# Transfers of block 2 respaced, q of batch 3 in two places, q's turn moved within its slot, and the last pair's sums and reads rerouted in an attention and MLP kernel

## The chip, the cores and the metric

The kernel runs on one core of one Trainium2 chip. The metric is the device time of the whole launch in microseconds; lower is better. The engines are named as in the profile: PE (TensorE) multiplies matrices, PEld is its weight load, DVE is VectorE, ACT is ScalarE, POOL is GpSimd, SP is SyncE, whose queue issues nearly all transfers here ("SPq"). Each engine works through its own list of instructions in the order in which the program put them; a wait at the head of a list holds all that is behind it.

## The reference

Everything is float32. There are 8 batches with 8 heads, 576 tokens and a head size of 64.

```python
kv  = einsum('bhsd,bhse->bhde', k, v)
out = einsum('bhsd,bhde->bhse', q, kv)
x   = out / sqrt(mean(out*out, -1) + 1e-6) * g_norm      # per head
x   = x.transpose(0, 2, 1, 3).reshape(4608, 512)
h   = x @ w_in                                            # 512 x 2048
g   = maximum(0.01 * h, h)
return g @ w_out                                          # 2048 x 512
```

## The kernel before, in words

The 4608 rows of x are worked through in nine blocks of 512 tokens (`NB` = 9, `NT` = 512). Blocks 0 and 1 have forms of their own. Blocks 2 to 8 all have the same form, in which both products are done by Strassen's method, at two levels where it pays, so that sums of operands on DVE and POOL take the place of matmuls.

**Slots.** A block from 2 on is a loop over four parts of the hidden size (`c`) and seven products of each (`t`), 28 slots, `slot = 7 * c + t`. A slot takes about 3.3 us of PE. It issues, in this order: one step of the first product h (`h_steps`, `product_h_two`), then at `t == 0` the tail of the part before (`h_before`: the sums that make g, the leaky ReLU on ACT and the sums of g, `sums_of`), then one step of the second product o (`go_o`, with a lag), then pieces of the tail of the last batch (`late`) and of the attention for the next block (`a_steps`), then up to two queued loads (`load_some`). What was put off with `put_off` runs at a later slot's start. The order on each engine is pinned to this order.

**A step of h.** Each step multiplies into two banks of PSUM, and its result is added by DVE or copied by ACT into `qs`, a region of the tile `w1_all`. A bank is used again two steps later, so that a result has about one slot to be taken out. The steps of one part are 1, 2, 6, 5, 7, 3, 4.

**Weights of h.** They lie in DRAM as sums made in block 1 and are read through a ring of five places in `w1_all` (`read`, line 748): after a step the read for the step five later is issued. One read is 128 x 896 floats (448 KB).

**Weights of o.** The sums of w_out lie in DRAM too (`w2_dram`). `sides_w2` makes and writes them in block 1; `read_side` (line 944) reads 128 x 512 floats into one of three places in the tile `pairs`, in the order of `side_reads`; `load_four` (lines 911 to 913) reads quarters for the two-level form and, in block 2, has POOL sum them and writes the sums back. The second product of block 1's last part, `product_o(3)`, runs during block 2's slots 4 to 13 and, when it has ended, issues three side reads and two times `load_four` at once. A pair of parts (`product_o_pair`) follows it.

**Attention of the next batch.** While block i runs, batch i + 1 is prepared. The four pairs of heads of q come in one after another: four transfers each (line 172), a turn on DVE (line 467, a transpose of 128 x 576) into the tile `qT`, and then the next pair's load. For batches from 3 on all q pairs use a single place, `q_in`, so that a load waits for the turn of the pair before. `attention_kv` multiplies k and v; the tail (`tail_of`, `outputs`, `both_outputs`) multiplies qT with kv into `o_ps`, and DVE and ACT normalise it into xT. The tables `FINE_2` (for block 2), `FINE_3` (for block 3) and `FINE_SLOTS` say how many steps of the attention follow each slot:

```python
    FINE_SLOTS = {4: 1, 8: 2, 11: 1, 15: 3, 16: 1, 17: 2, 18: 2, 19: 9}
    FINE_3 = {4: 1, 8: 2, 11: 1, 15: 3, 16: 1, 18: 2, 19: 3, 20: 9}
    FINE_2 = {2: 1, 5: 2, 8: 1, 11: 3, 16: 1, 17: 2, 18: 2, 19: 9}
```

In blocks 3 to 6 the four turns are the first step at slots 4, 8, 11 and 15. In block 2 they are at slots 2, 5, 8 and 11.

**The end.** The last pair of parts of block 8 has one level only and follows `LAST_PLAN` ("1a 2a 1b 2b 6a 6b 5a 5b ..."). It needs the four sums of g (`gs`) of the last part, which POOL makes (line 644, called from `sums_of`).

Of the kernel before, what the change touches and what calls it, by code (L numbers as in the profile page):

```python
# [24 lines left out]
def kernel(  # L25
# [112 lines left out]
        return ins.tile([P, J, D], F32, tag=f"{name}_in", name=f"{name}_in")  # L138

    def q_tile(b, p):  # L140
        if p % 2 and b < 3:
            return w1_all[:, 2 * NC * NW:]
        return ins.tile([P, T * D], F32, tag="q_in", name="q_in", bufs=1)

# [2 lines left out]
    def load_some(n=1):  # L147

        while to_load and n > 0:
            b, p, what = to_load.popleft()  # L150
            load_pair(b, p, what)
            n -= 1
# [306 lines left out]
    def attention(b, apart=True, fine=False):  # L459

        qT = qTs[b] = work.tile([P, NP, S], F32, tag="qT", name="qT")
        beside = b > KV_BESIDE
        kv_ps = None if beside else kv_tiles()

        def turn(p):
            q_in = q_ins.pop((b, p))
            in_turn(nc.vector.transpose(
                qT[:, p, :].rearrange("p (t s) -> p s t", s=T),
                q_in.rearrange("p (s d) -> p s d", d=D)[:, :, :32]))

        def load_q(p):
            n = NP * b + p + (1 if b > 2 else 2)
            if apart and n < NP * B and (b != 2 or n <= NP * 3):
                put_off(b > 2, lambda: to_load.appendleft((n // NP, n % NP, "q")))

        for m in range(2):
            turn(2 * m)
            load_q(2 * m)
            yield
            turn(2 * m + 1)  # L480
            load_q(2 * m + 1)
            if m:
                yield
            if kv_ps:
                attention_kv(b, m, [t[:, m, :] for t in kv_ps])
            if not apart and m == 0:
                for p in (2, 3):
                    load_pair(b, p)
            elif apart and not beside:
                load_kv(b + m, 2 - 2 * m)  # L490
            yield
            if apart:
                if m and kv_ps:
                    copy_kv(b, kv_ps)
                yield
        if not apart:
            copy_kv(b, kv_ps)
            yield
        kv = [(None, None), (None, None)]
        if KV_BESIDE <= b < B - 1:  # L500
            kv = [(None, 0), (None, 1)] if b == KV_BESIDE else \
                [(None, 0) if b == KV_BESIDE + 1 else (0, None), (1, None)]
        tails = [tail_of(b, max(i * NT, b * S), min((i + 1) * NT, (b + 1) * S), fine, kv[i - b])
                 for i in (b, b + 1)]
        last_tails[b] = tails[1]
        yield from tails[0]
# [133 lines left out]
            round_w(j)  # L640


    def add(eng, out_, a, b_, minus=False, pinned=False):
        ins = eng.tensor_tensor(out_, a, b_, op=ALU.subtract if minus else ALU.add)  # L644
        if pinned or steady:
            pin(ins)
# [23 lines left out]
    def sides_w2(n):  # L670

        c = n % NC
        b11, b12 = w2_sb[0][c][:, :, :N2], w2_sb[0][c][:, :, N2:]
        b21, b22 = w2_sb[1][c][:, :, :N2], w2_sb[1][c][:, :, N2:]

        def sums(i):
            t = (t12, t34)[i]
            if n >= NC:  # L680
                pin(nc.sync.dma_start(t, w2_dram[c][i]))
                return
            if i == 0:
                add(nc.gpsimd, t[:, 0], b12, b11, True)
                add(nc.gpsimd, t[:, 1], b22, t[:, 0], True)
            else:
                add(nc.gpsimd, t[:, 0], b22, b12, True)
                add(nc.gpsimd, t[:, 1], b21, t12[:, 1], True)
            if (n, i) == (NC - 1, 1):

                writes.append((w2_dram[c][i], t))
            else:
                pin(nc.sync.dma_start(w2_dram[c][i], t))
        return {1: b11, 2: b21, 3: b22, 5: t12[:, 0], 6: t12[:, 1], 7: t34[:, 0],
                4: t34[:, 1]}, sums
# [156 lines left out]
    def sums_of(c, to):  # L852

        g11, g21, g22, g12 = g_of(c)
        s1, s2, s3, s4 = (gpool.tile([P, 4, P], F32, tag=f"gs{i}", name=f"gs{i}")
                          for i in range(1, 5))
        to.update({1: g11, 2: g12, 3: s4, 4: g22, 5: s1, 6: s2, 7: s3})
        add(nc.gpsimd, s1, g21, g22)
        add(nc.gpsimd, s2, s1, g11, True)
        add(nc.gpsimd, s3, g11, g21, True)  # L860
        add(nc.gpsimd, s4, g12, s2, True)

    def product_h(c, w_sides, x_sides, to):

        g11, g21, g22, g12 = g_of(c)

        def done(i, bank):

            if i == 1:
                nc.scalar.copy(g11, bank)  # L870
            elif i == 5:
                nc.scalar.copy(g22, bank)
            elif i == 2:
                add(nc.vector, g11, bank, g11, pinned=True)
                relu(g11)
            elif i == 6:
                nc.scalar.copy(g21, bank)
            elif i == 3:
                add(nc.vector, g21, bank, g21, pinned=True)
                relu(g21)  # L880
            elif i == 7:
                add(nc.vector, g22, bank, g22, pinned=True)
                relu(g22)
            else:
                relu(g12, bank)

        yield from strassen((("ha", "hc"), ("hb", "hd"))[c % 2], lambda i, part, r: w_sides[i][:, part, r, :],
                            lambda i, part, r: x_sides[i][:, r, :], done)
        sums_of(c, to)

# [33 lines left out]
        put_off(3, sums)  # L926
        put_off(6, write)

    later, tick = [], 0

    def put_off(n, what):
        later.append((tick + n, what))
        later.sort(key=lambda x: x[0])

    side_reads = [(m + h, i) for m in range(NC, END, 2)
                  for i in ((5, 6, 7) if two_levels(m) else (6, 5, 7, 4)) for h in range(2)]
    side_at = {key: view(pairs, (16 + 4 * (at % 3)) * P, U, N2) for at, key in enumerate(side_reads)}
    to_read = collections.deque(side_reads)

    def read_side():  # L940
# [55 lines left out]
    def product_h_two(i, c, quarters, to, second):  # L996
# [46 lines left out]
        yield  # L1043
        for t in (g11, g12, g22, g21):
            relu(t)
        sums_of(n, to)

    def product_o(n, g_sides, os, finish):

# [10 lines left out]
        def done(i, bank):  # L1060
            key, fresh = into[i]
            to = os[key].rearrange("p u (v n) -> p (u v) n", v=2)
            if c == 0 and fresh:
                nc.scalar.copy(to, bank)
            else:
                add(nc.vector, to, bank, to)
            if c == NC - 1 and i in (2, 7, 3, 4):
                finish(key, os[key])

            if i == 5:  # L1070
                sums(0)
            elif i == 4:
                sums(1)


        yield from strassen((("oa", "oc"), ("oc", "oa"))[n % 2], lambda i, part, r: g_sides[i][:, 2 * r + part, :],
                            lambda i, part, r: w_sides[i][:, r, :], done)
        if n == NC - 1:
            for _ in range(3):
                read_side()  # L1080
            for m in range(2):
                load_four(NC + m)

    PLAN = "1a 1b . 5a 5b 6a 6b 3a 3b 7a 7b A D ."
    LAST_PLAN = "1a 2a 1b 2b 6a 6b 5a 5b 7a 7b 3a 3b 4a 4b"
# [1 line left out]
    def product_o_pair(n, g_sides, os, finish):  # L1087
# [36 lines left out]
        for step in (PLAN if two else LAST_PLAN).split():  # L1124
# [39 lines left out]
                           stop=(r == 1), skip_group_check=True)  # L1164
            if i in (5, 6, 7, 4):
                read_side()
            if h == 0:
                yield
                continue
# [107 lines left out]
    A_SLOTS = (2, 3, 5, 8, 10, 11, 13, 14, 15, 17)  # L1277

    TAIL_SLOTS = {1: 1, 4: 1, 5: 2, 6: 1, 8: 2}
    FINE_SLOTS = {4: 1, 8: 2, 11: 1, 15: 3, 16: 1, 17: 2, 18: 2, 19: 9}  # L1280
    FINE_3 = {4: 1, 8: 2, 11: 1, 15: 3, 16: 1, 18: 2, 19: 3, 20: 9}
    FINE_2 = {2: 1, 5: 2, 8: 1, 11: 3, 16: 1, 17: 2, 18: 2, 19: 9}
    SUM_SLOTS = {22: 2, 23: 1, 24: 1}

    LAG = 2
# [18 lines left out]
    for i in range(1, NB):  # L1304
        one = i == 1
        steady = not one
        late = last_tails.pop(i, iter(()))
        a_steps = attention(i + 1, fine=not one) if i + 1 < B else iter(())
        os = {}
        for c in range(NC):  # L1310
# [7 lines left out]
            for t in range(7):  # L1318
                slot = 7 * c + t
                tick += 1  # L1320
                while later and later[0][0] <= tick:
                    later.pop(0)[1]()
                go(h_steps, 1)
                if t == 0:
                    go(h_before, 3)
# [9 lines left out]
                if not one:  # L1335

                    go(late, TAIL_SLOTS.get(slot, 0))
                    go(a_steps, {2: FINE_2, 3: FINE_3}.get(i, FINE_SLOTS).get(slot, 0))
                    if i + 1 < NB:
                        if slot == 22:  # L1340
                            x_sides, new_quarters, sums, inner = sides_x(i + 1)
# [2 lines left out]
                            inner(0)  # L1344
                        elif slot == 26:
                            inner(1)
                    load_some(2 if i == 2 else 1)

                if c % 2 == 0 and now - 2 in begun and 2 <= t < 6:
                    inner_g(now - 2 + t % 2, 3 if t < 4 else 2)  # L1350
# [5 lines left out]
                if one:  # L1356
# [12 lines left out]
                        in_line = False  # L1369
                    if slot in A_SLOTS:  # L1370
                        go(a_steps, 1)
                    load_some(2 if i == 2 else 1)
                    if slot == 24:
                        go(a_steps)
                        x_sides, new_quarters, sums, inner = sides_x(i + 1)
# [13 lines left out]
            if one:  # L1389
                go(h_steps)  # L1390
            elif now == END - 1:
                for _ in range(2):
                    go(h_steps, 1)
                    go_o()
                go(h_steps)
            else:
                h_before = h_steps
            if c == NC - 1 and i + 1 < NB:
# [39 lines left out]
```

## Time and profile before

| what | value |
|---|---|
| median of 3 runs | 921.16 us (918.72 to 923.7) |
| the profiled execution's own time | 920.61 us |
| its span, first to last instruction | 918.9 us |
| granted TensorE clock | 1.000 |
| PE busy | 906.7 us, 99% of the span |
| DVE, ACT, POOL busy | 581.6, 329.2, 474.8 us |
| mean rate of all transfers | 224 GB/s, 206.25 MB |

The table of waits shows, for each engine and line, how long it stood idle and what ended that. The timeline shows instructions in order of time: start, duration, engine, line, operation, tiles out<-in, shape, count, and in brackets the idle time of the engine before it and what ended it. A row of SPq is a transfer's issue, not its duration.

### The profile page before, as it was taken

The page shows a single profiled execution, that of the slowest core. Times are in us where ns is not written, and L with a number is a line of the kernel's source. Part 1 is how long each engine was busy: PE and PEld are TensorE (multiplying, and loading weights), DVE is VectorE, ACT ScalarE, POOL GpSimd, SP SyncE. Part 2 cuts the span into 40 slices and gives each one's busy share as a digit, 9 for nine tenths or more (in the row PEclk, how much of TensorE's full clock was granted, in tenths as well). Part 3 has the DMA queues.
Part 4 walks back from the last instruction along what each step waited for, and adds up shares of the span by engine and source line. Part 5 has one row for each costly group of instructions (what it writes and reads, how often), then busy time and mean ns, then how long its engine had stood idle before and what let it go on. Part 6 is the DMA issues. An engine that isn't in the chain of part 4 may idle for free.

```text
span 918.9 us, 18517 instructions
## 1 busy us (share of the span) xinstructions
PE 906.7 (99%) x7148; PEld 774.8 (84%) x7148; DVE 581.6 (63%) x882; ACT 329.2 (36%) x645; POOL 474.8 (52%) x588
## 2 busy tenths in 40 slices
PE   8999999999999999999999999999999999999998
PEld 4444448888988989898999999999989899999997
DVE  5876985565865667665775576656755664555442
ACT  5454524332234232434333343334242524232420
POOL 2000246977539674656355653566266736673622
PEclk9999999999999999999999999999999999999999
DMA  8999918954799678967897679766876667667613
GB/s 255 216 246 235 246 61 263 363 182 154 245 281 359 192 243 273 293 206 245 230 293 234 211 235 290 251 196 212 235 235 203 184 203 234 195 196 229 209 41 103
DMA packets 102615, 206.25 MB, mean 224 GB/s; under 512 B 11264, under 2 KB 46976, under 8 KB 102528
## 3 DMA queue, kind: packets, MB, share of 16 engines
q1 hardware_dynamic: 98592, 199.50, 72.7%
q10 hardware_dynamic: 3488, 4.39, 1.4%
q8 instruction: 57, 0.93, 0.4%
q0 software_dynamic: 448, 1.18, 0.3%
q14 instruction: 30, 0.25, 0.1%
HBM read 176.72 MB, written 28.31 MB: 223 GB/s over the span
## 4 chain that ended last, share of the span: by engine, by line
PE 89%; DMA 4%; DVE 4%; issue 1%; POOL 1%; ACT 0%; SPq 0%; DVEq 0%; ACTq 0%; POOLq 0%
PE o_a L121 18%; PE o_c L121 15%; PE h_hd L121 9%; PE h_hc L121 9%; PE h_ha L121 9%; PE h_hb L121 8%; PE o_acc L121 6%; PE h_ps L121 6%; PE o_ps L121 3%; PE h_a L121 2%; PE h_b L121 2%; DMA q_in<-in_q_dram 1%; DVE g L644 1%; PE h_d L121 1%; PE h_c L121 1%; PE kv_ps L121 1%
## 5 line engine op out<-in xcount | busy, mean ns | idle before, releaser
L644 POOL TENSOR_TENSOR gs<-g 128x512 f32<-128x512 f32 x64 | 83.3, 1303 | 164.4 <-DVE w_all L644 79.6
L644 POOL TENSOR_TENSOR w_all<-w_all 128x512 f32<-128x512 f32 x28 | 56.2, 2008 | 120.2 <-ACT w_all L1021 114.1
L121 PE MATMUL o_a<-pairs,gs 128*128 128x256 f32 x480 | 114.0, 380 | 0.7 <-POOL gs L644 0.7
L836 ACT ACTIVATE g<-g 128x512 f32<-128x512 f32 x124 | 75.2, 629 | 74.6 <-DVE g L644 74.5
L644 DVE TENSOR_TENSOR g<-g,w_all 128x512 f32<-128x512 f32 (+1 forms) x84 | 92.6, 1102 | 6.9 <-POOL w_all L644 1.2
L121 PEld LDWEIGHTS o_a<-pairs,gs 128*128 128x128 f32 x480 | 86.9, 190 | 10.6 <-POOL gs L644 0.9
L644 DVE TENSOR_TENSOR o_all<-o_a,o_all 128x512 f32<-128x512 f32 (+1 forms) x53 | 35.4, 668 | 82.2 <-PE o_a L121 81.6
L644 DVE TENSOR_TENSOR o_all<-o_c,o_all 128x512 f32<-128x512 f32 (+2 forms) x80 | 46.5, 581 | 53.0 <-PE o_c L121 40.3
L1021 ACT COPY w_all<-h_hc 128x512 f32<-128x512 f32 x42 | 25.0, 596 | 116.2 <-PE h_hc L121 116.2
L121 PE MATMUL o_c<-pairs,gs 128*128 128x256 f32 x272 | 64.2, 380 | 1.8 <-DMA pairs<-w 1.8
L644 DVE TENSOR_TENSOR w_all<-h_ha,w_all 128x512 f32<-128x512 f32 x42 | 28.8, 686 | 52.0 <-PE h_ha L121 51.9
L121 PE MATMUL o_a<-w,g 128*128 128x256 f32 x248 | 58.8, 379 | 0.0
L121 PE MATMUL h_ps<-xT,w_all 128*128 128x512 f32 (+1 forms) x136 | 58.1, 571 | 0.3 <-DVE w_all L271 0.3
L121 PE MATMUL o_acc<-w,g 128*128 128x512 f32 x128 | 57.6, 594 | 0.0
L121 PE MATMUL o_c<-w,gs 128*128 128x256 f32 x240 | 56.6, 379 | 0.0
L644 POOL TENSOR_TENSOR pairs<-w 128x512 f32<-128x512 f32 x4 | 5.3, 1334 | 98.6 <-ACT cut L258 98.6
L644 DVE TENSOR_TENSOR g<-w_all 128x1024 f32<-128x1024 f32 x28 | 35.1, 1254 | 33.2 <-ACT w_all L1021 33.2
L121 PEld LDWEIGHTS o_c<-pairs,gs 128*128 128x128 f32 x272 | 49.5, 190 | 7.5 <-POOL gs L644 2.0
L121 PEld LDWEIGHTS h_ps<-xT,w_all 128*128 128x128 f32 x136 | 25.4, 190 | 29.0 <-issue 25.6
L121 PEld LDWEIGHTS o_acc<-w,g 128*128 128x128 f32 x128 | 24.2, 190 | 30.5 <-issue 29.9
L121 PEld LDWEIGHTS o_a<-w,g 128*128 128x128 f32 x248 | 45.0, 190 | 5.0
L121 PEld LDWEIGHTS o_c<-w,gs 128*128 128x128 f32 x240 | 43.5, 190 | 4.7
(262 smaller groups left out, 2292.4 us busy)
## 6 DMA issues: line engine op xcount, KB each, us to landing
w_all<-w SPq DMA_DIRECT2D x196, 448.0 KB, 4.4
pairs<-w SPq DMA_DIRECT2D x99, 256.0 KB, 3.7
v_in<-in_v_dram SPq DMA_DIRECT2D x29, 288.0 KB, 4.9
k_in<-in_k_dram SPq DMA_DIRECT2D x28, 288.0 KB, 4.9
q_in<-in_q_dram SPq DMA_DIRECT2D x48, 144.0 KB, 5.5
q_in<-in_q_dram SPq DMA_DIRECT2D x48, 140.0 KB, 5.8
w<-stage SPq DMA_DIRECT2D x12, 512.0 KB, 4.3
out_dram<-o_all SPq DMA_DIRECT2D x24, 256.0 KB, 5.6
```

The lines of the kernel that those rows point to most:

```text
L121: pin(nc.tensor.matmul(*args, **kw))
L644: ins = eng.tensor_tensor(out_, a, b_, op=ALU.subtract if minus else ALU.add)
L836: nc.scalar.activation(t, t if src is None else src, func=AF.Prelu, alpha=SLOPE)
L1021: nc.scalar.copy(q[:, at], bank)
```

## The change

It has five parts.

- **Block 2's transfers.** One queued load goes out in each slot, where block 2 had two. The three side reads and the two `load_four` that followed `product_o(3)` are issued within it, after its products 5, 7, 3 and 4. Both writes of the last part's sums of w_out to DRAM are put off to slot 4; one of them was issued in block 1's order before.
- **q of batch 3.** Its pair 1 gets a place of its own, in `w1_all`, which later holds part of `qs`. It is loaded in block 1, so that pairs 0 and 1 are both there at block 2's start. `load_q` queues the next load at once, not a slot later. In block 2 the turns move to slots 2, 3, 8 and 12, the two rounds of `attention_kv` to slots 4 and 12, and the tail's outputs to slots 17 and 18.
- **Turn first.** The tables get a second half, whose steps run ahead of the slot's h step. In blocks 3 to 6 the turns of slots 8, 11 and 15 run ahead of the h step and the o step of these slots; the one of slot 4 is now the first thing of slot 5.
- **Sums of the last pair.** For the last part the four sums of g are made by DVE, two and two, with DVE's other work between them.
- **Reads of the last pair.** The last five side reads go to places in `w1_all` and are all issued after step 1b, where they went round the three places of `pairs`.

```diff
     def q_tile(b, p):
-        if p % 2 and b < 3:
+        if p % 2 and NP * b + p < NP * 3 + 2:
             return w1_all[:, 2 * NC * NW:]
...
         def load_q(p):
-            n = NP * b + p + (1 if b > 2 else 2)
-            if apart and n < NP * B and (b != 2 or n <= NP * 3):
-                put_off(b > 2, lambda: to_load.appendleft((n // NP, n % NP, "q")))
+            n = NP * b + p
+            n += 2 if n <= NP * 3 else 1
+            if apart and n < NP * B and n != NP * 3 + 2 or n == NP * 3 + 2 and p == 0:
+                to_load.appendleft((n // NP, n % NP, "q"))
...
-            if m:
+            if m or b == KV_BESIDE:
                 yield
...
-            if (n, i) == (NC - 1, 1):
+            if n == NC - 1:
                 writes.append((w2_dram[c][i], t))
...
-        add(nc.gpsimd, s1, g21, g22)
-        add(nc.gpsimd, s2, s1, g11, True)
-        add(nc.gpsimd, s3, g11, g21, True)
-        add(nc.gpsimd, s4, g12, s2, True)
+        eng = nc.gpsimd if c < END - 1 else nc.vector
+        if c == END - 1:
+            yield
+        add(eng, s1, g21, g22)
+        add(eng, s2, s1, g11, True)
+        if c == END - 1:
+            yield
+        add(eng, s3, g11, g21, True)
+        add(eng, s4, g12, s2, True)
...
+    side_at.update((key, view(w1_all, 4 * at * P, U, N2)) for at, key in enumerate(side_reads[-5:]))
...
+            if n == NC - 1:
+                if i in (5, 7):
+                    read_side()
+                elif i == 3:
+                    load_four(NC + 1)
+                elif i == 4:
+                    read_side()
+                    load_four(NC)
...
-        if n == NC - 1:
-            for _ in range(3):
-                read_side()
-            for m in range(2):
-                load_four(NC + m)
...
+            if not two and step == "1b":
+                for _ in range(5):
+                    read_side()
...
-    FINE_SLOTS = {4: 1, 8: 2, 11: 1, 15: 3, 16: 1, 17: 2, 18: 2, 19: 9}
-    FINE_3 = {4: 1, 8: 2, 11: 1, 15: 3, 16: 1, 18: 2, 19: 3, 20: 9}
-    FINE_2 = {2: 1, 5: 2, 8: 1, 11: 3, 16: 1, 17: 2, 18: 2, 19: 9}
+    FINE_SLOTS = {16: 1, 17: 2, 18: 2, 19: 9}, {5: 1, 8: 2, 11: 1, 15: 3}
+    FINE_3 = {16: 1, 18: 2, 19: 3, 20: 9}, {5: 1, 8: 2, 11: 1, 15: 3}
+    FINE_2 = {4: 2, 8: 1, 12: 1, 13: 1, 17: 1, 18: 2, 19: 9}, {2: 1, 3: 1, 12: 1}
...
+                go(a_steps, 0 if one else fine[1].get(slot, 0))
                 go(h_steps, 1)
...
-                    go(a_steps, {2: FINE_2, 3: FINE_3}.get(i, FINE_SLOTS).get(slot, 0))
+                    go(a_steps, fine[0].get(slot, 0))
...
-                    load_some(2 if i == 2 else 1)
+                    load_some()
...
             elif now == END - 1:
-                for _ in range(2):
-                    go(h_steps, 1)
+                for steps in (1, 1, 2, 1, 1):
+                    go(h_steps, steps)
                     go_o()
-                go(h_steps)
```

More of the change, by code (lines that the diff above doesn't have):

```diff
@@ L640, in first_attention, with put_off @@
             round_w(j)
+    later, tick = [], 0
+    def put_off(n, what):
+        later.append((tick + n, what))
+        later.sort(key=lambda x: x[0])
     def add(eng, out_, a, b_, minus=False, pinned=False):
@@ L888, in product_h @@
                             lambda i, part, r: x_sides[i][:, r, :], done)
-        sums_of(c, to)
+        yield from sums_of(c, to)
     more = consts.tile([P, 19, P], F32, name="more")
@@ L927, in load_four @@
         put_off(6, write)
[L929 to L933, printed above, removed]
     side_reads = [(m + h, i) for m in range(NC, END, 2)
@@ L1045, in product_h_two @@
             relu(t)
-        sums_of(n, to)
+        yield from sums_of(n, to)
     def product_o(n, g_sides, os, finish):
@@ L1306 @@
         steady = not one
+        fine = {2: FINE_2, 3: FINE_3}.get(i, FINE_SLOTS)
         late = last_tails.pop(i, iter(()))
@@ L1371 @@
                         go(a_steps, 1)
-                    load_some(2 if i == 2 else 1)
+                    load_some()
                     if slot == 24:
```

## The prediction

> **What bounds the kernel now.** I read the page first: PE is busy for 906.7 of 918.9 us at a granted clock of 1.000, and 89% of the chain that ended last is PE. The change removes no matmul: on PE only the two rounds of kv matmuls and the o_ps products of block 2 stand elsewhere. So all that it can gain is PE's idle time, and the second view is the table of what PE waited for, without the first 27 us.
>
> ```profile
> PE o_c L121 <- DMA pairs<-w: 1.8, 1, 1.8
> ...
> PE h_ha L121 <- DVE w_all L644: 1.4, 1, 1.4
> PE o_ps L121 <- DVE qT L467: 1.3, 2, 0.7
> ...
> PE o_a L121 <- POOL gs L644: 0.7, 1, 0.7
> ```
>
> Columns: total us, times, longest. These four are the whole price: 5.2 us, 0.57% of the run. The third view is the timeline around each. Two lie in block 2:
>
> ```profile
> 266.17 1.89 PE L121 MATMUL o_c<-pairs,g 128*128 128x256 f32 x8
> ...
> 267.27 1.26 DVE L467 STREAM_TRANSPOSE qT<-q_in 128x576 f32<-128x576 f32 x1 [4.64 <-DMA q_in<-in_q_dram]
> ...
> 269.50 0.49 PE L121 MATMUL h_ha<-xT,w_all 128*128 128x128 f32 x2 [1.43 <-DVE w_all L644]
> ...
> 276.10 1.39 SPq L944 DMA_DIRECT2D pairs<-w  x3
> ...
> 282.16 1.97 PE L121 MATMUL o_c<-pairs,gs 128*128 128x256 f32 x8 [1.79 <-DMA pairs<-w]
> ```
>
> In the first, DVE stood 4.64 us at the turn of batch 3's last q, behind which the results of h were queued. In the second, PE wanted a side read that was issued only at 276.10. Matmul ends are modelled, so I count from starts: 8 records of 0.216 us each from 266.17 end at 267.90, and the next started at 269.50: 1.60 us lost. The second is 1.96 likewise (6 records of 0.112 from 279.53, next at 282.16).
>
> The third group is in blocks 4 to 6, at slot 16; block 5:
>
> ```profile
> 568.77 0.55 DVE L644 TENSOR_TENSOR w_all<-h_hd,w_all 128x384 f32<-128x384 f32 x1
> ...
> 569.72 1.26 DVE L467 STREAM_TRANSPOSE qT<-q_in 128x576 f32<-128x576 f32 x1 [0.41 <-DMA q_in<-in_q_dram]
> ...
> 571.04 0.63 PE L121 MATMUL o_ps<-qT,kv 64*32 64x128 f32 x20 [0.56 <-DVE qT L467]
> ```
>
> The fourth is at the end, where PE waits for POOL's second sum:
>
> ```profile
> 897.16 0.28 DVE L644 TENSOR_TENSOR o_all<-o_hc,o_all 128x128 f32<-128x128 f32 x1
> ...
> 898.53 1.26 POOL L644 TENSOR_TENSOR gs<-gs,g 128x512 f32<-128x512 f32 x1
> ...
> 899.85 1.13 PE L121 MATMUL o_a<-pairs,gs 128*128 128x256 f32 x4 [0.70 <-POOL gs L644]
> ```
>
> **Part 1, the last q turn of block 2: -1.6 us.** Pair 1 of batch 3 is now loaded in block 1, so that block 2 loads two pairs where it loaded three. Pair 2 is issued after the first turn (240.8) and pair 3 after the turn at slot 8. DVE is through slot 8's o result at 257.66 before; one turn (1.25) no longer stands ahead of it there, so the third turn ends at about 257.7 and pair 3 is issued then. A q pair lands 5.5 us after issue in the median and 8.7 at most: 263.2 to 266.4. Its turn is first in slot 12. The results behind it (0.68 and 0.55 us) must be out when slot 14's h starts, which is 267.9 without the stall: the turn must start by 267.9 - 1.23 - 1.26 = 265.4. Bytes: from 240.4 to 258 SP now issues some 6.2 MB (q, seven ring reads, two k and v pairs, two writes of 512 KB, out, two side reads), and 295 GB/s was moved in that stretch before, 413 in the best 4 us of block 2. At 295 the 6.2 MB and pair 3's 0.57 MB are through at 240.4 + 22.9 = 263.3, 2 us in time. What is late next is nothing at slot 14: the kv round behind slot 12's h has its k and v from slots 4 and 5.
>
> **Part 2, the side reads: -1.96 us.** They go out behind slots 7, 8 and 13, some 20 us ahead of their use; even the third, behind pair 0 of batch 4, needs only half its lead. `load_four` goes out behind slots 11 and 13 and its POOL sums at slots 14 and 16, ahead of POOL's add into qs at slot 14. If the first of them lands late, that add waits. By the bytes (2.4 MB from 258, at 295) it lands at about 266, before POOL needs it (270.05 before, about 268 now). Nothing, unless it lands after 270.
>
> Late next at that place would be POOL's last gs, done at 281.94 before; but PE's first product there uses the sums of the part before, done at 262.2, and the next one's first sum was done at 278.14. Nothing.
>
> **Part 3, turns first in blocks 3 to 6: -1.7 us.** Each load of the next pair goes a slot earlier (turn and queueing), and at slot 11 it passes the four `load_four` reads on SP. In block 5 the last turn follows the sum that ends at 568.26, not the two h results behind it: it ends at about 569.5, before PE asks at 570.04. The turn delays those results by 1.26 us to about 570.8; their bank is wanted at slot 17, 572.80. The stalls go: 1.3 in the table, 0.08 in block 4, and by starts up to 1.9. I take 1.7.
>
> The new wait is DVE's for q. Earliest is slot 8: in block 4 the pair lands at 446.46 and DVE comes there at 445.8, so DVE stands 0.7 us; behind it the results of slot 8, due at slot 10, 452.08; done by 449.1. Covered by 3 us.
>
> **Part 4, the end: -0.8 us.** DVE is free of the 1b results at 897.44. Two sums on DVE at 0.69 each (the row of g, 128x512 from SBUF, 0.69) end at 898.8; PE asks at 898.98 (898.53 and 4 records of 0.112). POOL has nothing left then. The one o_c result behind them is 1.4 us later (899.5); its bank is wanted at 901.7. The stall was 0.87 by starts; between 0.7 and 0.87 goes. The five reads were never waited for: 0.
>
> The Trainium skill speaks against this part ("Perfetto Trace Analysis", Optimizing Scalar/DVE Operations): VectorE and GpSimd share a port, so that moving work between them might not help. By it this part would be 0; here POOL's last other add ends at 893.2, so that there is nothing to share the port with.
>
> **Part 5, what block 2's start adds: +0.3 us.** At slots 2 and 3 two turns now stand one behind the other, ahead of the results of slot 4. They come after this:
>
> ```profile
> 234.53 5.14 DVE L431 TENSOR_TENSOR sum<-sq 128x192 f32<-128x192 f32 x2 [0.71 <-ACT sq L429]
> 239.59 1.24 DVE L467 STREAM_TRANSPOSE qT<-q_in 128x576 f32<-128x576 f32 x1
> ```
>
> Two small sums took 5.14 us, while POOL ran adds without a gap from 228.6 to 238.9. So the second turn ends at 242.1. ACT's copy of h_hd of slot 3 overwrites part of that q place and now waits for it (0.5 us, 242.6); PE wants this bank in slot 5, at 241.24 + 1.2 for the kv round that moved ahead = 242.45. Between 0 and 0.4; 0.3. The DVE results of slot 4 follow at 243.3, due at 244.94.
>
> The Trainium skill ("SBUF — State Buffer", Who interferes with whom) has the pair of ports held for one instruction of whichever engine came first. By it the sum would have waited only for the add that ran until 234.82, both turns would end near 238 and this term be 0; the row shows a wait through four adds.
>
> **What costs nothing.** Block 1 gets one q pair more and other places for POOL's sums and SP's writes. PE waited for nothing there (no row of the table lies between 140 and 226 us), and the cover is wide: the sums of g that PE takes up at 217.7 were done at 210.2. The write that held SP until 233.62, waiting for POOL, goes behind the ring reads of slots 0 to 2, so that these leave some us earlier; PE waited for none of them. If the cover is gone, PE pays one for one.
>
> **Sum.** 1.6 + 1.96 + 1.7 + 0.8 - 0.3 = 5.76 us, taken as 5.8; by the bounds 1.6 + 1.96 + 1.3 + 0.7 - 0.4 = 5.2 to 1.6 + 1.96 + 1.9 + 0.87 = 6.3. The profiled execution took 920.61, 0.55 below the median of 921.16. Against it: 914.8 us, 914.3 to 915.4.
>
> **Rivals.**
>
> *The transfers collide again, or DVE's start of block 2 does (0.27).* For: DMA engines are at a share of 0.91 from 240 to 258 already, and more now goes there. Pair 3 after 265.4 costs PE one for one; at the longest landing, 8.7, and an issue at 258.5 that is 1.8, more than part 1's 1.6, which is then gone: 916.4. If POOL's unbroken adds begin 2 us later, because the order of its sums in block 1 is another, part 5 is 2.3: 916.8; both, 918.4. Against: bytes and POOL's rows above.
>
> *It doesn't do what it says (0.05).* The stalls are only handed on to the next wait, as PE comes earlier to the same reads: 918.6 to 922.
>
> *Slower (0.06): the turns hold DVE.* In blocks 3 to 6 three turns now stand ahead of h results. Their place is slot 8, where the pair has the shortest lead. It decides from the point where q lands after 449.5 in block 4 (11.3 us after its issue at 438.19; 8.3 there before): then 449.5 + 1.26 + 1.37 passes 452.08, and each us costs one in each of four blocks. Landing 15 us after issue, 3.7 late, costs 14.8 against the 5.8: 930. It passes the break-even at 1.5 late. Against: 8.7 is the longest landing of q in the run.
>
> **How the numbers follow.** Forecast 0.62, at 914.8. Range 911.9 to 919: below, 914.3 less the 2.4 by which the lowest run shown lies under its median; above, the first rival's 918.4 and some of the second's. Some 0.12 is left out. About 0.5% (4.6 us) is what a measurement here can tell from no change; the forecast's 5.8 is just over it, and the first rival's cases are within. Faster 0.62, same 0.32, slower 0.06.
>
> **What would show it.** Right: the four rows of the first table gone, and PE busy 906.7 in a span near 913; the turn at slot 12 of block 2 with no wait for q over 1 us; at the end o_a following o_hc without a gap. Wrong: a row of PE waiting for ACT or DVE w_all near 242 (part 5 too small), a row for q or w_all near 268 (part 1), PE waiting for h results at slot 10 of blocks 3 to 6 (the slower rival), or pairs<-w still waited for.

## The result, and the profile after

The changed kernel took 914.65 us (median of 6 runs, 912.53 to 915.9) where the kernel before took 921.88 (6 runs on the same chip, 918.72 to 924.85): a ratio of 0.9918, with a 95% interval of 0.9893 to 0.9943. The profiled execution of the changed kernel took 914.69, with a span of 913.0 us, 5.9 less than before, at the same granted clock of 1.000. PE is busy for 905.2 us (906.7 before). By the medians the change is worth 7.2 us, by the two profiled executions 5.9; what follows accounts for the 5.9. One execution of one experiment, its profiled one (the first try with the end's sums on POOL), ran at a granted clock of 0.851 and took 1036.94 us; it is left out below.

The forecast was 914.8. Its sum was right, its terms were not: one was too small by 1.3 us, and a wait of 1.2 us that it had set at nothing ate nearly all of the difference. The table of what PE waited for, first for the changed kernel:

```profile
PE idle_ps L121 <- DVE group L307: 1.5, 1, 1.5
PE h_hb L121 <- ACT w_all L1342: 1.0, 1, 1.0
PE kv_ps L121 <- DMA pairs<-in_v_dram: 0.7, 1, 0.7
...
PE o_ps L121 <- DMA v_in<-in_v_dram: 0.3, 1, 0.3
```

All four rows that the prediction priced are gone. Two are new: h_hb waiting for ACT, and o_ps waiting for v. The first and the third line belong to the first 27 us, as before. Where the time went is read from the timeline, from the start of the first matmul of slot 0 of each block to the next one's:

| stretch, us | before | after | difference | predicted |
|---|---|---|---|---|
| block 2 | 93.69 | 91.80 | -1.89 | -3.26 |
| blocks 3 to 6 | 385.98 | 382.94 | -3.04 | -1.7 |
| block 7 | 93.25 | 93.25 | 0 | 0 |
| block 8 to the span's end | 119.64 | 118.66 | -0.98 | -0.8 |

**Block 2's new wait.** The timeline of the changed kernel from 264 to 278, with only the rows of the chain:

```profile
264.87 0.41 SPq L925 DMA_DIRECT2D more<-w  x1
...
265.90 1.26 DVE L467 STREAM_TRANSPOSE qT<-q_in 128x576 f32<-128x576 f32 x1 [3.69 <-DMA q_in<-in_q_dram]
...
267.74 0.30 PEld L121 LDWEIGHTS h_ha<-xT,w_all 128*128 128x128 f32 x2 [0.40 <-DVE w_all L651]
...
271.19 2.21 POOL L651 TENSOR_TENSOR more<-more 128x128 f32<-128x128 f32 x4 [7.91 <-DMA more<-w]
...
273.35 1.27 POOL L651 TENSOR_TENSOR w_all<-w_all 128x512 f32<-128x512 f32 x1
...
274.65 1.23 DVE L651 TENSOR_TENSOR g<-g,w_all 128x1024 f32<-128x1024 f32 x1 [2.94 <-POOL w_all L651]
...
275.97 0.48 ACT L1342 COPY w_all<-h_hb 128x384 f32<-128x384 f32 x1 [3.05 <-DVE g L651]
...
276.50 0.94 PE L121 MATMUL h_hb<-stage,w_all 128*128 128x128 f32 x6 [1.03 <-ACT w_all L1342]
```

Read from the bottom: PE wants the bank of h_hb; ACT can't copy it out, since the copy overwrites what DVE's sum of g still has to read; that sum waits for POOL's add into w_all; and that add stands on POOL behind four small sums, for whose operands POOL waited 7.91 us. These are the sums of `load_four`. Their read was issued at 264.87 and landed at 271.12. PE itself waits for none of that data here. By starts PE lost 1.19 us. The last q turn, at 265.90, is half a microsecond past the 265.4 that the prediction had as its limit, and PE lost 0.16 there (the row of PEld at 267.74).

**Blocks 3 to 6.** DVE and PE of the changed kernel in block 5, around the last turn:

```profile
564.61 0.68 DVE L651 TENSOR_TENSOR o_all<-o_all,w_all 128x512 f32<-128x512 f32 x1
565.21 1.25 DVE L467 STREAM_TRANSPOSE qT<-q_in 128x576 f32<-128x576 f32 x1
566.31 0.68 DVE L651 TENSOR_TENSOR w_all<-h_hc,w_all 128x512 f32<-128x512 f32 x1
```

```profile
566.32 0.83 PE L121 MATMUL h_hb<-stage,w_all 128*128 128x128 f32 x6
567.08 0.67 PE L121 MATMUL o_ps<-qT,kv 64*32 64x128 f32 x32
```

The turn now follows the sum without a wait for q, is done at 566.46, and PE takes up qT at 567.08 with no idle time ahead of it.

**The end.** The same two sums on DVE, and PE behind them:

```profile
892.42 0.68 DVE L651 TENSOR_TENSOR gs<-g 128x512 f32<-128x512 f32 x1
...
893.14 0.69 DVE L651 TENSOR_TENSOR gs<-gs,g 128x512 f32<-128x512 f32 x1
...
893.60 0.61 PE L121 MATMUL o_hc<-pairs,gs 128*128 128x128 f32 x4
...
894.04 1.03 PE L121 MATMUL o_a<-pairs,gs 128*128 128x256 f32 x4
```

The second sum ends at 893.83, and o_a follows o_hc after 4 x 0.11 us, without a gap.

### The profile page after: what moved, and what is told of

It is laid out like the page before. It is cut to its first block, busy times and chain, and to the rows that moved or that the text cites. A ratio compares the mean times of both kernels' runs of the same rounds, so it can differ in the third digit from the quotient of the medians.

```text
span 913.0 us, 18526 instructions
## 1 busy us (share of the span) xinstructions
PE 905.2 (99%) x7148; PEld 774.7 (85%) x7148; DVE 582.9 (64%) x886; ACT 329.8 (36%) x645; POOL 469.1 (51%) x584
## 3 DMA queue, kind: packets, MB, share of 16 engines
q0 software_dynamic: 448, 1.18, 0.3%
## 4 chain that ended last, share of the span: by engine, by line
PE 93%; DMA 3%; DVE 2%; POOL 1%; issue 0%; ACT 0%; SPq 0%; DVEq 0%; ACTq 0%; POOLq 0%
PE o_a L121 19%; PE o_c L121 15%; PE h_hc L121 9%; PE h_hd L121 9%; PE h_ha L121 9%; PE h_hb L121 9%; PE o_acc L121 6%; PE h_ps L121 6%; PE o_ps L121 3%; PE h_a L121 2%; PE h_b L121 2%; PE h_d L121 1%; PE h_c L121 1%; PE kv_ps L121 1%; DMA pairs<-in_v_dram 1%; DMA v_in<-in_v_dram 1%
## 5 line engine op out<-in xcount | busy, mean ns | idle before, releaser
L121 PE MATMUL o_a<-pairs,gs 128*128 128x256 f32 x472 | 111.9, 380 | 0.0
L1028 ACT COPY w_all<-h_ha 128x512 f32<-128x512 f32 x42 | 24.8, 591 | 66.7 <-PE h_ha L121 66.7
```

Of the source, the lines that this page charges most:

```text
L121: pin(nc.tensor.matmul(*args, **kw))
L1028: nc.scalar.copy(q[:, at], bank)
```

## The experiments

Times are medians, beside those of the kernel before on the same chip (921.5 to 921.7). Since a few tenths of a microsecond decide, each kernel is read by the lengths of its stretches in its profiled execution.

| kernel | block 2 | blocks 3 to 6 | block 8 to end | span | median | ratio to before, 95% interval |
|---|---|---|---|---|---|---|
| turns behind the h step | 90.79 | 384.78 | 118.66 | 913.4 | 915.88 | 0.9929 (0.9904 to 0.9954) |
| last turn behind | 91.65 | 384.78 | 118.66 | 914.8 | 916.27 | 0.9936 (0.9914 to 0.9958) |
| load a slot later | 92.64 | 385.22 | 119.12 | 916.1 | 916.99 | 0.9959 (0.9939 to 0.9978) |
| turns alone, on the kernel before | 92.14 | 382.95 | 119.67 | 914.9 | 918.94 | 0.9952 (0.9932 to 0.9971) |
| sums of four put off | 89.89 | 382.94 | 118.67 | 911.5 | 913.21 | 0.9913 (0.9882 to 0.9943) |
| and k, v of batch 4 together | 89.65 | 382.95 | 118.66 | 911.0 | 912.7 | 0.9896 (0.9865 to 0.9928) |
| the same once more | 89.68 | 382.94 | 118.67 | 916.0 | 912.8 | 0.991 (0.9886 to 0.9935) |
| the same, end on POOL | 89.65 | 382.95 | 119.63 | 912.8 | 913.51 | 0.9911 (0.9894 to 0.9928) |
| reads at the end | 90.40 | 382.94 | 118.66 | 911.2 | 913.29 | 0.9891 (0.987 to 0.9913) |
| reads at the end, in the ring | 91.36 | 382.94 | 118.66 | 912.8 | 915.75 | 0.9935 (0.9916 to 0.9955) |
| three q pairs in block 2 | 95.01 | 382.95 | 118.66 | 915.9 | 917.79 | 0.9954 (0.9931 to 0.9977) |

Blocks 3 to 6 repeat to 0.02 us between executions with the same code there, and the end to 0.03 us, but for one end (the load a slot later, below). Block 2 does not repeat; the last section has what is known of it.

### Block 2: is it POOL's sums?

```diff
-        put_off(3, sums)
-        put_off(6, write)
+        put_off(6, sums)
+        put_off(9, write)
```

> The changed kernel, with POOL's sums of the four-read load in block 2 put off by 6 slots where it was 3, and their write by 9 where it was 6, so that POOL doesn't stand at the read that lands at 271.1 and its add into w_all comes before. Theory (the late read, through POOL's add, DVE's fourth sum of g and ACT's copy of h_hb, makes PE wait 1.19 us at slot 16 of block 2): the row of PE waiting for ACT w_all goes, block 2 takes 90.5 to 90.8 us where it took 91.80, and the time is 1.0 to 1.2 us below the changed kernel's 914.65, if PE, which is then earlier, doesn't stand the longer for v of batch 4 (up to 0.5 given back: 0.7). Rival (DVE's own line, with the q turn of 265.9 in it, makes the fourth sum late): the row stays with 0.8 to 1.2 us and the block keeps 91.6 to 91.8.

The row of ACT w_all is gone, and so is that of v of batch 4. DVE, ACT and PE at slot 16, without POOL in the way:

```profile
271.94 1.23 DVE L651 TENSOR_TENSOR g<-g,w_all 128x1024 f32<-128x1024 f32 x1
...
273.25 0.48 ACT L1342 COPY w_all<-h_hb 128x384 f32<-128x384 f32 x1 [0.21 <-DVE g L651]
...
275.44 0.83 PE L121 MATMUL h_hb<-stage,w_all 128*128 128x128 f32 x6
```

Counted from the block's start, the fourth sum starts 3.1 us sooner, and PE has its bank 1.7 us ahead of use. Block 2 took 89.89, less than the theory's 90.5 to 90.8, since in this execution q landed 2.5 us sooner as well (263.75), and v only 0.1 us after the first of its products had started. That left it open whether the q turn had a part in the wait. Two other runs answer it. In the kernel with only the last turn behind, below, the last q turn of block 2 starts 38.8 us after the block's start, and PE lost 1.18 at slot 16, as in the changed kernel. In the fastest version with the end on POOL, where the sums are put off, it starts at 38.6, and block 2 takes 89.65 with no row for ACT. It was POOL.

```diff
-                       for kind in (("kv",) if b <= 3 else "kv"))
+                       for kind in (("kv",) if b <= 4 else "kv"))
```

> The kernel with the four-read load's sums put off, and k and v of batch 4 loaded together a slot earlier, as k and v of batch 3 are. Theory (v of batch 4 is the last transfer of block 2 and PE waits 0.3 to 0.5 us for it): that row goes as well, block 2 takes 90.1 to 90.3 us and the time is 1.5 to 1.7 us below 914.65. Rival (the DMA queues are full there, so that v pushed ahead makes another read late): another row for a DMA takes its place and block 2 takes 90.5 us or more.

89.65, and no row of v in o_ps. That is 0.24 less than with the sums put off alone. The two blocks agree up to the products of k and v (57.66 us after the block's start in both). In the kernel without this edit v landed 0.11 us after the first of these products had started, a wait too short for a row, and together they take 1.44 us, where they take 1.21 here. In the changed kernel v cost 0.48, but no pair of kernels here shows this edit by itself to be worth more than 0.24.

> The fastest version so far once more, unchanged, to see whether its time holds: 912.0 to 913.5 us, block 2 at 89.6 to 90.2 us, no row of PE waiting for ACT w_all, for pairs<-w or for v of batch 4. If block 2's transfers land up to 1 us later in this execution, 90.5 to 91 with one such row.

Block 2 took 89.68 and the median is 912.8. The profiled execution has a span of 916.0 all the same, since PE stood elsewhere, at 70 and 92 us:

```profile
PE kv_ps L121 <- DMA v_in<-in_v_dram: 3.2, 2, 2.7
```

That lies ahead of block 2, which starts 5.0 us later than in its twin with the same code (231.50 against 226.46); from there on the two agree. By starts the two waits make 3.6 us of the 5.0; the rest is lost right behind them, where the granted clock was 0.67 from 95 to 100 us; why is open.

### Block 2: the reads' place, or the queue?

```diff
-            if n == NC - 1:
-                if i in (5, 7):
-                    read_side()
-                elif i == 3:
-                    load_four(NC + 1)
-                elif i == 4:
-                    read_side()
-                    load_four(NC)
...
+        if n == NC - 1:
+            for _ in range(3):
+                read_side()
+            for m in range(2):
+                load_four(NC + m)
```

> The changed kernel, with block 2's three side reads and the two four-read loads back at the end of the product, one behind the other. Theory (two transfers fewer ahead don't help, the reads' place was the wait): PE waits 1.4 to 2.2 us for pairs<-w again at slot 18, and the wait for ACT's w_all at slot 16 goes with the late read's sums (1.19 less): block 2 takes 92.0 to 92.8 us where it took 91.80. Rival (with a q pair less and the ring left out, the reads come early enough from there too): no such row, and block 2 takes 89.9 to 90.6.

The rival was right, and the theory behind part 2 wrong. SP and PE of this kernel:

```profile
270.71 1.55 SPq L951 DMA_DIRECT2D pairs<-w  x3
...
276.26 0.83 PE L121 MATMUL h_hd<-stage,w_all 128*128 128x128 f32 x6
...
276.93 1.89 PE L121 MATMUL o_c<-pairs,gs 128*128 128x256 f32 x8
```

Issued where the kernel before has them in its order, the three reads now go out at 270.71 and not at 276.10, and the first has landed at 276.19, 0.74 ahead of its use. The rest of the change is in place here: a q pair less in block 2 with its turns, one load in a slot, and the writes put off. Which of these brought the reads forward is not told apart. With the four-read loads at the end too, their sums come after POOL's add into w_all, so that the wait for ACT is gone as well: 90.40, 1.40 less than the changed kernel.

```diff
-    side_at.update((key, view(w1_all, 4 * at * P, U, N2)) for at, key in enumerate(side_reads[-5:]))
```

> The kernel with block 2's side reads and loads of four back at the end of the product, and the five last side reads in their old places in the ring as well. Theory (the wait for pairs<-w in the kernel before came from the queue on SP, where a third q pair and its followers stood ahead of the read, not from the ring's place): block 2 takes 90.2 to 90.7 us, with no row of o_c waiting for pairs<-w, as with the reads at the end and no ring (90.40). Rival (the ring's place comes free late and holds the read): the read is issued after 273, o_c waits 0.5 to 2 us for it, and block 2 takes 91 to 92.4.

(The five reads that are issued together after step 1b overwrite ring places that are still to be read here, so that the last products run on other data; the work is the same.) The reads were issued at 271.93, and o_c lost 0.17 us to the first, which landed at 277.50, too little for a row. The late transfer was v of batch 4 (1.42 by starts), which makes the block 91.36: above the theory's range and inside the rival's. But the rival's signs, an issue after 273 and 0.5 us or more lost in o_c, did not come. The ring's place was not the wait.

```diff
-        if p % 2 and NP * b + p < NP * 3 + 2:
+        if p % 2 and b < 3:
...
-    FINE_2 = {4: 2, 8: 1, 12: 1, 13: 1, 17: 1, 18: 2, 19: 9}, {2: 1, 3: 1, 12: 1}
+    FINE_2 = {2: 1, 5: 2, 8: 1, 11: 3, 16: 1, 17: 2, 18: 2, 19: 9}, {}
```

(With `load_q`, the yield and the two loads in a slot as they were.)

> The changed kernel, with batch 3's q back in its old places: one slot in turn, pair 1 loaded in block 2 and not in block 1, so that three q pairs go through block 2, the turns where they stood, two loads in a slot; the side reads and the load of four stay where the change put them. Theory (the third pair is what made the last turn late, and with the reads now ahead of it, it lands later yet): DVE stands 4 us or more at the turn in slot 12 again, PE waits 1.6 to 4 us at slot 14 (268 to 270), and block 2 takes 93.0 to 96 us. Rival (the reads' places were the whole gain of the block): block 2 takes 91.6 to 92.2.

```profile
268.63 1.26 DVE L467 STREAM_TRANSPOSE qT<-q_in 128x576 f32<-128x576 f32 x1 [5.95 <-DMA q_in<-in_q_dram]
```

DVE stands 5.95 us, PE 3.29, and the block takes 95.01, longer than before the change. So block 2 gained by the q pair that went to block 1, together with the places of the turns and the single load in a slot, which this kernel takes back with it and no run separates; and the two parts depend on each other: without it, with the reads ahead, the block is worse than before.

### Blocks 3 to 6: the turn's place, or the load?

```diff
-    FINE_SLOTS = {16: 1, 17: 2, 18: 2, 19: 9}, {5: 1, 8: 2, 11: 1, 15: 3}
+    FINE_SLOTS = {4: 1, 8: 2, 11: 1, 15: 3, 16: 1, 17: 2, 18: 2, 19: 9}, {}
```

> The changed kernel, with the q turns of blocks 3 to 6 put back behind the h step of their slot (slots 4, 8, 11, 15), while the loads are still queued at once. Theory (the turn's place in DVE's line is what blocks 3 to 6 gained by): each of these blocks gets its waits at slot 16 back and takes 96.5 to 97.0 us from start to start where the changed kernel takes 96.0, some 2.0 to 3.0 us in all; the rows of PE, and of its weight loads, waiting for DVE qT come back; about 917 us. Rival (the earlier load alone was the gain): the blocks stay at 96.0 to 96.2 and the time within 0.7 us of the changed kernel's 914.65.

```diff
-    FINE_SLOTS = {16: 1, 17: 2, 18: 2, 19: 9}, {5: 1, 8: 2, 11: 1, 15: 3}
+    FINE_SLOTS = {15: 3, 16: 1, 17: 2, 18: 2, 19: 9}, {5: 1, 8: 2, 11: 1}
```

(`FINE_3` likewise in both.)

> The changed kernel, with only the turn of slot 15 put back behind the h step in blocks 3 to 6; the turns of slots 5 and 8 stay first. Theory (only the last turn had PE waiting, the two h results of 0.55 us each stand ahead of it): nearly all that the first of these kernels loses is lost here too, 2.0 to 3.0 us, blocks of 96.5 to 97.0. Rival (the gain is spread over all three places, or comes from q landing sooner): under 1.2 us, blocks under 96.4.

Both kernels take 384.78, so the turns at slots 5, 8 and 11 give nothing and the last one gives it all: 1.84 us, 0.46 in each block. That is less than the 2.0 that either theory asked for. The other 1.20 stays with the earlier load. By blocks, 3 to 6, the place is worth 0.47, 0.45, 0.46 and 0.46, the load 0, 0.14, 0.50 and 0.56.

```diff
-                to_load.appendleft((n // NP, n % NP, "q"))
+                if b > 3:
+                    put_off(1, lambda: to_load.appendleft((n // NP, n % NP, "q")))
+                else:
+                    to_load.appendleft((n // NP, n % NP, "q"))
```

> The changed kernel, with the q loads of blocks 3 to 6 queued a slot later, as before the change, while the turns stay first in their slot. The first two experiments gave 1.84 of the 3.04 us of these blocks to the last turn's place, so that 1.20 is left to the earlier load; the two need not add up. Theory (the turn can't start before q has landed, which in the kernel before was 0.0 to 0.4 us before the turn: place and load help only together): blocks 3 to 6 take 385.0 to 386.0 us together, nearly all of the 3.04 gone, and DVE shows idle time at the turn of slot 15 with DMA q_in as its releaser. Rival (the two add up): 384.0 to 384.4, that is 1.2 of it gone.

385.22: of the 3.04 us, 2.28 are lost, not 1.2. Block 4's last turn of this kernel:

```profile
469.77 0.68 DVE L654 TENSOR_TENSOR o_all<-o_all,w_all 128x512 f32<-128x512 f32 x1
471.73 1.26 DVE L467 STREAM_TRANSPOSE qT<-q_in 128x576 f32<-128x576 f32 x1 [1.27 <-DMA q_in<-in_q_dram]
```

Put first, the turn finds no q and stands. Place and load are worth 1.84 and 2.28 when either is taken away, but 3.04 together: each needs the other. By blocks this kernel takes 97.10, 96.80, 96.29 and 95.03, where the kernel before took 96.53, 96.62, 96.99 and 95.84: in blocks 3 and 4 the turn put first without the earlier load is worse than no change. (The 0.46 us that this execution's end is longer lie behind PE's last matmul.)

```diff
+                if not one:
+                    go(a_steps, {2: FINE_2, 3: FINE_3}.get(i, FINE_SLOTS)[1].get(slot, 0))
                 go(h_steps, 1)
```

(On the kernel before, with the tables of the changed kernel for blocks 3 to 6 and the load queued at once there.)

> The kernel before, with the q turns of blocks 3 to 6 first in their slot and their loads queued at once, and nothing else of the change. Theory (blocks 3 to 6 gain by this alone, and block 2 and the end by the other parts): blocks 3 to 6 take 382.9 to 383.1 us together where before took 385.98 and the changed kernel 382.94; block 2 stays near 93.7, the end near 119.6; 3.0 us below the kernel before. Rival (part of that gain comes from what block 2 hands over, k and v of batch 4 and the reads being ahead): blocks 3 to 6 take 383.8 us or more.

382.95, as in the changed kernel, and a median 2.8 below that of the kernel before: these blocks gain by this part alone and owe block 2 nothing. But block 2, which is as in the kernel before, took 92.14 and not 93.69. Its last turn:

```profile
266.41 1.26 DVE L467 STREAM_TRANSPOSE qT<-q_in 128x576 f32<-128x576 f32 x1 [3.35 <-DMA q_in<-in_q_dram]
```

q landed at 266.29 here and at 267.15 in the profile of before, and PE came 0.53 later: by starts it lost 0.2 there, so that most of the 1.6 us that part 1 was to remove was not there in this execution. The other wait of block 2, at the o_c of slot 18, stayed, and its row names POOL:

```profile
PE o_c L121 <- POOL gs L647: 1.6, 1, 1.6
```

POOL's last sum of g ended at 281.08 and the first side read landed at 281.00, as close together as in the kernel before (281.94 and 282.02). That this product does not need that sum is shown by the changed kernel: there it starts at 278.84, and POOL's last sum ends at 282.66. The read is what held it.

### The end

```diff
-        eng = nc.gpsimd if c < END - 1 else nc.vector
+        eng = nc.gpsimd
```

> The changed kernel, with the last pair's sums of g on POOL again (the yields between them kept). Theory (the two sums on VectorE are what the end gained by): from block 8's start to the span's end takes 119.5 to 119.7 us where the changed kernel takes 118.67 and the kernel before 119.64, and the row of PE waiting for POOL gs comes back with 0.7 to 0.9; about 915.6 us. Rival (the yields, that is, the sums' place among the steps, made the gain): the end stays at 118.7 to 119.0.

The median of the five other executions is 916.01, 1.4 above the changed kernel's, with a ratio of 0.9924 (0.9896 to 0.9951) to the kernel before: too wide to tell. The edit was made again on the fastest version:

> The fastest version so far (sums of the load of four put off, k and v of batch 4 together), with the last pair's sums of g on POOL again. Its profile is to show what the first try of this edit left open. Theory (the engine of the two sums is what the end gained by): block 8's start to the span's end takes 119.5 to 119.7 us where that version takes 118.66, the row of PE waiting for POOL gs stands at 0.7 to 0.9, and the time is 0.9 to 1.0 above that version's of the same call. Rival (the yields made the gain): 118.6 to 119.0, and no difference.

```profile
PE o_a L121 <- POOL gs L651: 0.7, 1, 0.7
```

119.63 against 118.66 and 118.67: 0.97 us, and the row of before is back. The medians of the two kernels, measured side by side on one chip, are 913.51 and 912.8. The yields by themselves gave nothing.

## Why the prediction was right, and where it was wrong

| term | predicted | measured | by |
|---|---|---|---|
| 1: the last q turn of block 2 | -1.6 | -1.43 | starts at 267.7 |
| 2: the side reads | -1.96 | -1.96 | the row is gone |
| 2: `load_four`, "nothing, unless it lands after 270" | 0 | +1.19 | landed at 271.12 |
| v of batch 4 | not named | +0.48 | landed at 286.0 |
| 3: turns first | -1.7 | -3.04 | blocks 3 to 6 |
| 4: the end | -0.8 | -0.98 | block 8 to end |
| 5: block 2's start | +0.3 | 0 | no wait at slot 5 |

What is left of block 2's 1.89 is 0.17, spread over waits under 0.2. The sum was to be -5.76 and is -5.91. That it came so close is luck: 1.34 us too little in part 3 was offset by 1.19 and 0.48 that the sum did not have.

**Part 1** held, at the late end of its range: q was to land between 263.2 and 266.4 and landed at 265.88, 0.5 past the limit for the turn. The estimate of 263.3 by bytes was 2.6 us too early, and the sign that the prediction had given for being right, no wait for q over 1 us at this turn, did not come: DVE stood 3.69 us there, and PE lost only 0.16 by it. The three-pairs kernel bears out the mechanism, and the turns-alone kernel that its price in one profile, 1.6, was partly chance.

**Part 2** is where a step failed, in two ways. The wait for pairs<-w went, but not because the reads were put ahead: with one q pair less and the rest of the change, the same reads from the old place in the order are in time by 0.74. And the step "by the bytes (2.4 MB from 258, at 295) it lands at about 266" took the transfer to go out when the program comes to it. SP's list has waits of its own: the row of SPq has the read at 264.87, after SP had stood 2.3 us at a ring read ahead of it, until an earlier ring read had landed (263.59), and it took 6.25 us from there. The prediction had named what is behind it ("ahead of POOL's add into qs") and the 270 from which it costs, and then trusted the landing. So the move of `load_four` cost 1.19 and the move of the side reads gained nothing that the end of the product wouldn't have given.

**Part 3** had the mechanism and the wrong size. The 1.7 came from PE's row (1.3, 2 times) and from starts in blocks 4 to 6. The stall stands in PE's weight loads too, where the table of waits of the kernel before has it for all four blocks; the prediction did not use this row:

```profile
PEld o_ps L121 <- DVE qT L467: 2.5, 4, 0.9
```

Block 3 has no row of PE at all and still lost 0.47. The lengths of the blocks would have said it: 96.53 to 96.99 for blocks of like work, 96.03 when nothing waits.

**Part 4** held: 0.97 by the comparison on one version. The Trainium skill ("Perfetto Trace Analysis", Optimizing Scalar/DVE Operations) warns that moving operations between the two engines might not help, since they share a port, and the prediction put that at 0. Here POOL had nothing to do after 888.31, the sums started on DVE at 892.42, and the move was worth the whole stall.

**Part 5** cost nothing: ACT's copy of h_hd ran from 241.87 to 242.35 and PE wanted the bank at 242.63, with 0.28 to spare where the prediction had it 0.15 short.

**The rivals.** "The transfers collide again" came true in kind and at a place that it did not name: by POOL at slot 16, not by q at slot 14 or DVE at slot 3. Nothing of the slower rival was seen; in block 4 the earliest q landed at 444.82 and DVE stood 1.58 us for it, without anyone waiting for DVE.

**A faster version** follows from this: the changed kernel with the sums put off and k and v of batch 4 together took 912.7 and 912.8. Against the kernel before that is 0.9896 (0.9865 to 0.9928) and 0.991 (0.9886 to 0.9935). Its two traces, and that of the variant with the end on POOL, have block 2 at 89.65 to 89.68, 2.1 us below the changed kernel's. By the medians it is 1.9 below the changed kernel, and those intervals overlap; the traces show that block 2 is shorter, not that every execution is (one span was 911.0, the other, with the waits ahead of block 2, 916.0).

## What to carry to other kernels

When a transfer is moved, ask who waits for it first, and what stands behind that engine in its list: a read that PE itself does not wait for can hold PE through three other engines. The two landings estimated from bytes came out 2.6 and 5.1 us too early here; for the second, the list that issues the transfer had waited for an earlier one to land. Take the lead from rows of the same queue, not from the rate. A stall must be priced from the lengths of like stretches, or from the weight loads' rows together with the matmuls', and what stands behind a late transfer is one draw from a spread, not a constant.

## What the runs showed of the hardware that was not expected

**Two small sums on DVE took 1.74 or 5.20 us.** At the start of block 2 DVE makes two sums of 128x192 while POOL adds without a gap. In the changed kernel:

```profile
234.52 5.03 DVE L431 TENSOR_TENSOR sum<-sq 128x192 f32<-128x192 f32 x2 [0.71 <-ACT sq L429]
239.47 1.25 DVE L467 STREAM_TRANSPOSE qT<-q_in 128x576 f32<-128x576 f32 x1
```

In the second execution of the fastest version, with POOL as busy (its rows there follow):

```profile
239.68 1.74 DVE L431 TENSOR_TENSOR sum<-sq 128x192 f32<-128x192 f32 x2 [0.71 <-ACT sq L429]
241.34 1.25 DVE L467 STREAM_TRANSPOSE qT<-q_in 128x576 f32<-128x576 f32 x1
```

```profile
238.58 1.28 POOL L651 TENSOR_TENSOR gs<-g 128x512 f32<-128x512 f32 x1
239.81 1.40 POOL L651 TENSOR_TENSOR gs<-g,gs 128x512 f32<-128x512 f32 x1
241.17 1.40 POOL L651 TENSOR_TENSOR pairs<-w,w 128x512 f32<-128x512 f32 x1
```

In 13 traces the pair took 4.69 to 5.20 us ten times, and 1.74, 1.76 and 2.58 in the other three. The Trainium skill ("SBUF — State Buffer", Who interferes with whom) has the shared ports held for one instruction of the engine that came first; it says so of VectorE's two-port modes, and of a VectorE instruction with two inputs in SBUF, like these sums, that it contends with GpSimd's reads. A short one agrees with that (two of POOL's adds beside it take 1.40, not 1.27), the ten long ones do not. What decides it is open; that a port is the cause is argued, not shown.

It matters off its own engine. The turns follow these sums, and the next q is issued after the turn. In the changed kernel the first q of block 2 is issued 14.4 us after the block's start, and the last lands at 39.5. With the sums put off, in an execution with a sum of 1.76, these are 11.1 and 37.0; in one with 4.96, 14.3 and 38.6. How the sums reach the last landing is open, since the last q pair is issued 31.8 us after the block's start in all three.

The long sums are not why block 2 differs between runs of like code. Its four executions in the changed kernel and its three variants of blocks 3 to 6 took 90.79 to 92.64, and all four had them (4.75 to 5.03). They differ by the landing of the first read of `load_four`: at 44.3, 44.6, 44.8 and 46.1 us after the block's start, with 0.87, 1.18, 1.19 and 2.00 us lost at slot 16. With the sums put off and k and v together block 2 took 89.65, 89.65 and 89.68, whether the sums took 2.58, 4.96 or 1.74: in these three, taking the wait away also took away the spread.
